# Moving the front's share, one wait and one PSUM place beside the first half of a plain MLP

## The chip, the cores and the metric

The kernel runs on one core of a Trainium2 chip, in fp32. The metric is the device time in microseconds. "Before" is the median of three runs; a profile is one further execution, whose time is given apart.

## The reference, cut to what matters

There are two stages. The first is a lightning attention with decay (4 batches, 8 heads, 768 positions, 64 wide); its output, with the heads side by side, is x (4, 768, 512). The second mixes x by a Fourier transform and applies an MLP:

```python
X = np.fft.fft(x, axis=1); X = np.fft.fft(X, axis=2)
u = x + np.real(X)
un = (u - mean(u)) / np.sqrt(var(u) + 1e-06)      # over the 512 channels
out = u + np.maximum(un @ w_ch1, 0.0) @ w_ch2     # 512 -> 2048 -> 512
```

The MLP's weights arrive as 64-bit floats.

## The kernel before

**The front.** For each batch b, `front(b)` runs `attn(b)` and then `fft_ln(b)`. The attention takes six chunks of 128 positions: k, q and v are loaded on SyncE's (SP's) DMA queue, transposed on TensorE (PE; L314, L319), scores are made (L338) and masked with the decay on VectorE (DVE; L343), the state is updated (L358, L363), and the output is made (L373, L379) and turned back (L395). `fft_ln` folds the sequence by symmetry on DVE (the sets fe and fo), transforms it on PE (L603, five groups, evicted by ScalarE (ACT) at L607), transforms the channels in three blocks `wide(1)`, `wide(2)`, `wide(0)` (L615 to L620), adds the result to x (L691 to L695), takes the statistics (L634, L635; L638 and L639 on GpSimd (POOL)) and normalizes (L655). Groups of 256 positions are named (b, g).

**The MLP.** The first four groups in `PLAIN`, (0,1), (0,2), (0,0), (1,1), are done plainly in `mlp`: their normalized rows are transposed on PE (L660), the first layer is L749 (a row is four matmuls into one PSUM place), its relu is L757 on ACT or L755 on DVE, the second layer is L763 over the pieces fc of the inner dimension. The first three groups are done in two halves of fc, 0 to 7 and then 8 to 15. After the first half the partial result is added into u (x in the code; L792, L793), at the end y is made (L796, L797) and stored (L736 on SP's queue, L738 on POOL's). Of the other eight groups (`LATE`) the normalized rows are transposed on DVE (L668) and stored to memory (L672, four DMAs for a tile, on SP), and u as well (L678). `late()` does them by a two-level Strassen form: first layer L1022, its first pair of groups being loaded into ur by `load_u` (L888, ACT's queue), with input sums sx (L923 to L929), then L1106 and L1180.

**The weights.** `load_weights` (L214 to L235) loads a raw piece of 512 columns on SP (L214) and makes fp32 of it: L226, L230, L232, L234, L235 on DVE, L225 and L228 on ACT. There are 32 pieces. The raw tiles share a ring of four ("hr") with the relu results. After the front, `combine_weights` makes the sums of weights that the Strassen form needs (L836 on DVE).

**PSUM.** While front and plain MLP run, `pa` has five places for the front, `pm` three for the MLP. In the first half of group (0,1) the two tiles of the second layer are started before the last piece fc = 7 and stay open (`split`), while the next group's first layer begins (`behind`).

**The order.** All of this is written as generators that yield an estimated cost in us after each step. `beside` and `weave` interleave two generators so that the second one advances in a set proportion to the first's costs; `chain` runs several one after the other. The program order so obtained is then adjusted by the tile scheduler, which gives instructions under `tc.high_priority` an earlier place and leaves those under `keep_in_program_order`. The stretch of interest is the end of the kernel function (L1360 to L1385): the first halves of the three groups run beside the second half of the weights' work and beside `fr`, the remaining front (the rest of attention and transform of batch 1, then batches 2 and 3). The last argument of the outer `beside` is the amount of `fr` that should pass during that first half. What remains of `fr` is then woven with `back`, the second halves and group (1,1). At `front_end.close()` the front's buffers are given up, and `load_u(0)` and the weight sums come beside the remainder of `back`. In `fft_ln(1)` (`b - 1 in LEADS` holds for b = 1 alone), a yield after the folds, 23.0, says how much other work is to pass before the transform L603 begins.

Of the kernel before, what the change touches and what calls it, by code (L numbers as in the profile page):

```python
# [17 lines left out]
ALU = mybir.AluOpType  # L18
# [59 lines left out]
def kernel(  # L78
# [12 lines left out]
    DM = H * D  # L91
# [8 lines left out]
    HM = DM // 2  # L100
# [39 lines left out]
    def new(pool, shape, tag, **kw):  # L140
        cnt[0] += 1
        return pool.tile(shape, F32, tag=tag, name=f"{tag}{cnt[0]}", **kw)

    def psum_a(shape):
        return new(pa, shape, "pa")

    def psum_m(shape):
        return new(pm, shape, "pm")
# [46 lines left out]
    NW = 2 * KO * DFF // WP  # L195
# [44 lines left out]
    def weights():  # L240

        for h in range(2):
            for f in range(h * DFF // 2, (h + 1) * DFF // 2, WP):
                for c in range(KO):
                    yield from load_weights(w1[:, c, f:f + WP], w1v[:, c, f:f + WP])
            for c in range(h * FO // 2, (h + 1) * FO // 2):
                yield from load_weights(w2[:, c, :], w2v[:, c, :])
# [47 lines left out]
    LEADS = (0,)  # L295
# [210 lines left out]
    def fold_a(b):  # L506
        for a, n in enumerate(BLK):
            yield from fold_x(b, a, n, 1, eo[b][a][1][0:n, 1, 0:DM], xn_[b, HC + a][0:n])
# [38 lines left out]
    def fold_b(b, sets):  # L547

        tt = nc.vector.tensor_tensor
        for a, n in enumerate(BLK):  # L550
            yield from fold_x(b, a, n, 0, xs[b, a][0:n], xs[b, HC + a][0:n])
            e, o = eo[b][a]
            nc.scalar.copy(e[0:n, :, HM:HM + 1], e[0:n, :, DM - 1:DM])

            am, bm = e[0:n, :, W:2 * W], o[0:n, :, W:2 * W]
            lo, hi = e[0:n, 0, 0:HM + 1], e[0:n, 1, 0:HM + 1]
            tt(am[:, 0, 0:HM + 1], lo, hi, op=ALU.add)
            tt(am[:, 1, 0:HM + 1], lo, hi, op=ALU.subtract)
            yield 0.8

            lo, hi = am[:, :, 0:QM], am[:, :, HM:QM:-1]
            tt(e[0:n, :, 0:QM], lo, hi, op=ALU.add)
            tt(e[0:n, :, QM:HM], lo, hi, op=ALU.subtract)
            yield 0.8
            lo, hi = o[0:n, 0, 1:HM], o[0:n, 1, 1:HM]
            tt(bm[:, 0, 1:HM], lo, hi, op=ALU.subtract)
            tt(bm[:, 1, 1:HM], lo, hi, op=ALU.add)
            yield 0.8
            lo, hi = bm[:, :, 1:QM + 1], bm[:, :, HM - 1:QM - 1:-1]
            tt(o[0:n, :, 0:QM], lo, hi, op=ALU.subtract)  # L570
            tt(o[0:n, :, QM:HM], lo, hi, op=ALU.add)
            yield 0.8
            sets.append((e, o))
        eo.pop(b)
# [3 lines left out]
    def fft_ln(b):  # L578
# [7 lines left out]
        if b in LEADS:  # L586
            yield from fold_a(b)
            yield from fold_b(b, sets)
            yield 2.0
        else:  # L590
            yield 1.0
            run(fold_a(b))
            yield 6.0 if b - 1 in LEADS else 3.0
            run((folds_apart if b > 1 else fold_b)(b, sets))
            yield 23.0 if b - 1 in LEADS else 9.0


        for i in (0, 1, 4, 2, 3):
            ps = psum_a([128, 2, NK])
# [133 lines left out]
    def store(b, T, y, cols=slice(0, DM)):  # L733
        if T < HC:
            row = S * b + 128 * T
            nc.sync.dma_start(out_low[row:row + 128, cols], y[:, cols])  # L736
        else:
            nc.gpsimd.indirect_dma_start(out=out_high,  # L738
                                         out_offset=row_of(2 + HC * (b + 1) + T - HC),
                                         in_=y[:, :], in_offset=None)  # L740

    def mlp(b, g, f0=0, f1=FO, behind=None):

        ut = uts[b, g]
        hr = []
        for fc in range(f0, f1):
            ps = psum_m([128, G * 128])
            for c in range(KO):
                nc.tensor.matmul(ps, lhsT=w1[:, c, 128 * fc:128 * fc + 128], rhs=ut[:, c, :],  # L749
                                 start=(c == 0), stop=(c == KO - 1))  # L750
            if fc % 4 == 0:
                hr.append(new(hp_, [128, 4, G * 128], "hr"))
            t = hr[-1][:, fc % 4, :]
            if fc % 2 and f1 == FO:
                nc.vector.tensor_scalar(t, ps, 0.0, None, op0=ALU.max)  # L755
            else:
                nc.scalar.activation(t, ps, AF.Relu)  # L757
            yield 1.7
            if f0 == 0:
                next(held.pop((b, g, fc), iter(())), 0)  # L760

        def second(ps, i, fc):
            return nc.tensor.matmul(ps, lhsT=hr[(fc - f0) // 4][:, fc % 4, 128 * i:128 * i + 128], rhs=w2[:, fc, :],  # L763
                                    start=(fc == f0), stop=(fc == f1 - 1))

        split = {}
        if behind is not None:
            for i in range(G):
                split[i] = psum_m([128, DM])
                for fc in range(f0, f1 - 1):  # L770
                    second(split[i], i, fc)
                    if fc % 4 == 3:
                        yield 3.4
                        if i == 1:
                            next(held.pop((b, g, FO), iter(())), 0)
                yield 2.6
                yield next(behind)
        for i in range(G):
            T = TT[g][i]
            if i in split:  # L780
                ps = split[i]
                tc.keep_in_program_order(second(ps, i, f1 - 1))
            else:
                ps = psum_m([128, DM])
            for fc in range(f0, f1) if i not in split else ():
                second(ps, i, fc)
                if fc % 4 == 3 and fc < f1 - 1:
                    yield 3.4
            u = xs[b, T]
            tt = nc.vector.tensor_tensor  # L790
            if f1 < FO:
                tt(u[:, 0:HM], ps[:, 0:HM], u[:, 0:HM], op=ALU.add)  # L792
                tt(u[:, HM:DM], ps[:, DM - 1:HM - 1:-1], u[:, HM:DM], op=ALU.add)  # L793
            else:
                y = new(up, [128, DM], "y", bufs=1)
                tt(y[:, 0:HM], ps[:, 0:HM], u[:, 0:HM], op=ALU.add)  # L796
                tt(y[:, HM:DM], ps[:, HM:DM], u[:, DM - 1:HM - 1:-1], op=ALU.add)  # L797
                store(b, T, y)
            yield 3.4 if i not in split else 0.8
# [517 lines left out]
    def front(b):  # L1317
        yield from attn(b)
        yield from fft_ln(b)

    def weave(lead, other, ratio):

        t_lead = t_other = 0.0
        for d in lead:
            t_lead += d
            while t_other < t_lead * ratio:
                d = next(other, None)
                if d is None:
                    return t_lead + sum(lead)
                t_other += d  # L1330
                yield d
            yield d
        return t_lead

    def run(gen):
        return sum(gen)

    def part(gen, n):
        for d in gen:
            yield d  # L1340
            n -= d
            if n <= 0:
                return

    def chain(gens):
        for g in gens:
            yield from g

    w = weights()
# [4 lines left out]
    def beside(lead, t, other, t_other):  # L1354
        return weave(lead, part(other, t_other), t_other / t)

    att1, mix = attn(1), fft_ln(0)
    att0 = attn(0)
    run(part(att0, 2.7))
# [3 lines left out]
    run(beside(mix, 24.0, beside(att1, 2.75 * t_chunk, w, 0.16 * NW), 0.16 * NW + 1.75 * t_chunk))  # L1363

    half = [[mlp(b, g, h * FO // 2, (h + 1) * FO // 2) for b, g in PLAIN[:3]] for h in range(2)]
    half[0][0] = mlp(*PLAIN[0], 0, FO // 2, half[0][1])
    fr = chain([att1, fft_ln(1)] + [front(b) for b in range(2, B)])
    t_rest, t_back = 3 * t_front - 5 * t_chunk, len(PLAIN) * t_mlp - 50.0
    t_half = 1.5 * t_mlp
    run(beside(beside(chain(half[0]), t_half, w, 0.5 * NW), t_half + 0.5 * NW, fr, t_rest * t_half / t_back))  # L1370
    run(w)
    back = chain(half[1] + [mlp(*PLAIN[3])])
    run(weave(fr, back, (t_back - t_half) / (t_rest - t_rest * t_half / t_back)))
    front_end.close()
# [44 lines left out]
```

## Time and profile before

| | |
|---|---|
| median of three runs | 789.23 us (788.49 to 789.73) |
| profiled execution, its own time | 789.55 us |
| its span in the profile | 787.6 us |
| mean granted TensorE clock | 0.992 |
| TensorE busy | 755.3 us, 96% |
| VectorE busy | 602.9 us, 77% |
| ScalarE busy | 230.7 us, 29% |
| GpSimd busy | 177.2 us, 22% |
| chain that ended last | PE 79%, DVE 9%, DMA 6% |

Columns of a group or a step in the trace: where it starts, how long it takes, the engine, the line, the operation, the tile written, the tiles read, shapes, and in brackets the engine's idle time ahead of it and what ended that. "x3" after a step stands for three instructions that follow one another and are shown as one. In the rows of tenths each of the 40 digits stands for 19.7 us of the span. The costliest single groups are L749 (119.6 us of PE) and L763 (115.4 us).

### The profile page before, as it was taken

The numbers are of one execution on the slowest core, as the hardware profiler recorded it, in microseconds if no ns is written. First come the engines' busy times: TensorE is split into PE (matmuls) and PEld (weight loads), VectorE is DVE, ScalarE is ACT, GpSimd is POOL, SyncE is SP. The second block draws the span as 40 slices with busy tenths as digits, with TensorE's granted clock in tenths as the row PEclk, the third lists the DMA queues.
The fourth block names the chain that finished last, engine by engine and source line by source line (L and its number), as shares of the span: only waits on it lengthen the run. The fifth ranks groups of instructions, "written<-read, shape, count | busy, mean of one in ns | idle before, by whom it ended". The sixth has DMA issues, their size and how long they took to land.

```text
span 787.6 us, 15005 instructions
## 1 busy us (share of the span) xinstructions
PE 755.3 (96%) x5784; PEld 648.0 (82%) x5784; DVE 602.9 (77%) x1167; ACT 230.7 (29%) x532; POOL 177.2 (22%) x202
## 2 busy tenths in 40 slices
PE   6888999999999999999995999999999999999997
PEld 5777876777685858678744889999999999999997
DVE  6999999767824686236597999878987699758984
ACT  3755444415531212231100221023411342024310
POOL 3223330001112014120003960350014100230013
PEclk9999999999999999999997999999999999999999
DMA  9979633246734037931243363776455455455442
GB/s 232 261 168 252 192 113 113 76 133 151 211 83 140 29 72 211 237 97 46 72 100 96 136 235 125 249 246 214 150 162 157 147 186 182 121 187 175 133 140 78
DMA packets 152957, 120.23 MB, mean 153 GB/s; under 512 B 114238, under 2 KB 114622, under 8 KB 152886
## 3 DMA queue, kind: packets, MB, share of 16 engines
q1 hardware_dynamic: 145824, 100.51, 45.9%
q0 software_dynamic: 4032, 12.99, 4.7%
q10 hardware_dynamic: 3030, 5.78, 2.1%
q8 instruction: 46, 0.75, 0.4%
q14 instruction: 25, 0.20, 0.1%
HBM read 88.04 MB, written 31.20 MB: 151 GB/s over the span
## 4 chain that ended last, share of the span: by engine, by line
PE 79%; DVE 9%; DMA 6%; issue 2%; ACT 1%; POOL 1%; SPq 1%; ACTq 0%; DVEq 0%; POOLq 0%
PE p L1180 21%; PE p L1106 17%; PE pm L749 11%; PE pm L763 9%; PE p L1022 6%; PE pa L338 3%; PE pa L379 3%; PE pa L603 3%; DMA raw<-in_moe_w_ch_dram 2%; PE pa L373 2%; DMA ur<-utd 1%; PE pa L358 1%; PE pa L314 1%; PE pa L319 1%; PE pa L395 1%
## 5 line engine op out<-in xcount | busy, mean ns | idle before, releaser
L749 PE MATMUL pm<-ut,w 128*128 128x256 f32 x512 | 119.6, 382 | 2.5 <-DVE x L793 1.4
L763 PE MATMUL pm<-w,hr 128*128 128x512 f32 x256 | 115.4, 595 | 0.0
L749 PEld LDWEIGHTS pm<-ut,w 128*128 128x128 f32 x512 | 94.3, 190 | 18.2 <-issue 3.7
L763 PEld LDWEIGHTS pm<-w,hr 128*128 128x128 f32 x256 | 46.7, 190 | 48.7 <-issue 48.0
L1201 POOL TENSOR_TENSOR y<-y,u 128x512 f32<-128x512 f32 x12 | 19.9, 1661 | 186.8 <-DVE y L1210 155.5
L1180 PE MATMUL p<-tx,sx 128*128 128x128 f32 x400 | 52.7, 275 | 0.0
L1180 PEld LDWEIGHTS p<-tx,sx 128*128 128x128 f32 x400 | 48.6, 192 | 0.0
L1115 DVE TENSOR_TENSOR ha<-p,ha 128x512 f32<-128x512 f32 x60 | 40.0, 683 | 8.3 <-PE p L1106 8.1
L310 POOL TENSOR_TENSOR kd<-k,decay 128x512 f32<-128x512 f32 x20 | 21.7, 1083 | 107.7 <-PE pa L358 71.7
L1186 ACT COPY y<-p 128x128 f32<-128x128 f32 x48 | 12.8, 266 | 103.6 <-PE p L1180 103.1
L343 DVE TENSOR_TENSOR sc<-pa,decay 128x512 f32<-128x512 f32 x48 | 31.0, 683 | 15.0 <-PE pa L338 14.6
L1188 DVE TENSOR_TENSOR y<-p,y 128x128 f32<-128x128 f32 x92 | 25.4, 283 | 16.1 <-PE p L1180 9.4
L1180 PE MATMUL p<-w,ha 128*128 128x128 f32 x288 | 37.4, 275 | 0.0
L638 POOL TENSOR_SCALAR ve<-mv 128x2 f32<-128x2 f32 x12 | 5.9, 491 | 133.5 <-DVE mv L635 133.2
L1115 DVE TENSOR_TENSOR hs<-p,hs 128x512 f32<-128x512 f32 x39 | 26.1, 683 | 12.0 <-PE p L1106 12.0
L1180 PEld LDWEIGHTS p<-w,ha 128*128 128x128 f32 x288 | 34.9, 192 | 0.1
L338 PEld LDWEIGHTS pa<-qT,kT 64*128 64x128 f32 x384 | 25.1, 193 | 12.0 <-ACT qT L321 6.7
L757 ACT ACTIVATE hr<-pm 128x256 f32<-128x256 f32 x44 | 16.7, 382 | 58.9 <-PE pm L749 54.8
L1106 PE MATMUL p<-sx,tx 128*128 128x128 f32 x264 | 33.9, 275 | 0.0
L338 PE MATMUL pa<-qT,kT 64*128 64x128 f32 x384 | 30.1, 292 | 2.9 <-ACT qT L321 2.9
L1106 PEld LDWEIGHTS p<-sx,tx 128*128 128x128 f32 x264 | 31.7, 192 | 0.0
L379 PE MATMUL pa<-sc,v 128*64 128x128 f32 x384 | 28.6, 282 | 1.1 <-DVE sc L343 1.1
(270 smaller groups left out, 1740.3 us busy)
## 6 DMA issues: line engine op xcount, KB each, us to landing
tx<-td SPq DMA_DIRECT2D x84, 256.0 KB
raw<-in_moe_w_ch_dram SPq DMA_DIRECT2D x32, 512.0 KB
tx<-sd SPq DMA_DIRECT2D x63, 256.0 KB
k<-in_k_dram SPq DMA_DIRECT2D x24, 256.0 KB
q<-in_q_dram SPq DMA_DIRECT2D x24, 256.0 KB
v<-in_v_dram SPq DMA_DIRECT2D x24, 256.0 KB
td<-tx SPq DMA_DIRECT2D x21, 256.0 KB
ud<-x SPq DMA_DIRECT2D x16, 256.0 KB
```

The lines of the kernel that those rows point to most:

```text
L310: nc.gpsimd.tensor_tensor(kd, kt, kpow, op=ALU.mult)
L338: mm(pss[hi][:, hp, :], lhsT=kT[HD[hi], hp, :], rhs=qT[HD[hi], hp, :], start=True, stop=True)
L343: nc.vector.tensor_tensor(t, pss[hi], decay[:, hi::2, :], op=ALU.mult)
L379: mm(po[HD[hi], hp, :], lhsT=vt[:, 2 * hp + hi, :], rhs=sc[hi][:, hp, :], start=(c == 0 and hp == 0), stop=(hp == HP - 1), skip_group_chec ...
L603: mm = nc.tensor.matmul(ps[:, n, :], lhsT=piece(a, i, n), rhs=cs[0:rows, a, i in (2, 3), n, :], start=(a == 0), stop=(a == 1))
L749: nc.tensor.matmul(ps, lhsT=w1[:, c, 128 * fc:128 * fc + 128], rhs=ut[:, c, :], start=(c == 0), stop=(c == KO - 1))
L763: return nc.tensor.matmul(ps, lhsT=hr[(fc - f0) // 4][:, fc % 4, 128 * i:128 * i + 128], rhs=w2[:, fc, :], start=(fc == f0), stop=(fc == f ...
L1022: nc.tensor.matmul(ps, lhsT=s2.A[a][:, kt, 128 * i:128 * i + 128], rhs=U[b][:, kt, :], start=(first and kt == 0), stop=(kt == 1), skip_gro ...
L1106: nc.tensor.matmul(ps[:, 128 * i:128 * i + 128], lhsT=ab[m][0][:, 128 * i:128 * i + 128], rhs=ab[m][1], start=(start and i == 0), stop=Tru ...
L1115: V.tensor_tensor(o, p, o, op=ADD)
L1180: nc.tensor.matmul(ps[:, 0:HM // 2], lhsT=ab[m][0][i], rhs=ab[m][1][:, i, :], start=(start and i == 0), stop=(i == HF // 2 - 1), skip_grou ...
L1188: V.tensor_tensor(o, ps[:, 0:HM // 2], o, op=ADD)
```

## The change

Four edits. The share of `fr` beside the first half of the MLP is raised by 15.0, the unit being the estimated us of the yields. The yield ahead of the transform of batch 1 goes from 23.0 to 27.0. The second of the two open tiles of group (0,1) gets a place in the front's PSUM pool `pa` in place of one in `pm`. And the partial sums of these two tiles (L792, L793) are given a higher priority in the scheduler.

```diff
@@ fft_ln, ahead of the transform
-            yield 23.0 if b - 1 in LEADS else 9.0
+            yield 27.0 if b - 1 in LEADS else 9.0
@@ mlp, the open tiles
-                split[i] = psum_m([128, DM])
+                split[i] = (psum_m, psum_a)[i]([128, DM])
@@ mlp, the partial sums
             if f1 < FO:
-                tt(u[:, 0:HM], ps[:, 0:HM], u[:, 0:HM], op=ALU.add)
-                tt(u[:, HM:DM], ps[:, DM - 1:HM - 1:-1], u[:, HM:DM], op=ALU.add)
+                with tc.high_priority(200) if i in split else ExitStack():
+                    tt(u[:, 0:HM], ps[:, 0:HM], u[:, 0:HM], op=ALU.add)
+                    tt(u[:, HM:DM], ps[:, DM - 1:HM - 1:-1], u[:, HM:DM], op=ALU.add)
@@ the share
-    run(beside(beside(chain(half[0]), t_half, w, 0.5 * NW), t_half + 0.5 * NW, fr, t_rest * t_half / t_back))
+    run(beside(beside(chain(half[0]), t_half, w, 0.5 * NW), t_half + 0.5 * NW, fr, t_rest * t_half / t_back + 15.0))
```

Lines after the edit in `mlp` stand one lower in the changed kernel (L793 for L792, L1023 for L1022).

## The prediction

> **What bounds the kernel now.** I read the page first, then TensorE's waits, then windows of 20 us, then the sequence of instructions at the two largest waits.
>
> ```profile
> span 787.6 us, 15005 instructions
> ...
> PE 755.3 (96%) x5784; PEld 648.0 (82%) x5784; DVE 602.9 (77%) x1167; ACT 230.7 (29%) x532; POOL 177.2 (22%) x202
> ...
> PE   6888999999999999999995999999999999999997
> ...
> PEclk9999999999999999999997999999999999999999
> ```
>
> TensorE (PE) is busy 96% of the span, so only its idle time, 32 us, and time at a lower clock can be won. One slice stands out, the twenty-second (about 413 to 433 us): half idle, and at 0.7 of the clock. TensorE's waits say which idle time is whose:
>
> ```profile
> PE p L1022 <- DVE sx L925: 8.3, 1, 8.3
> ...
> PE pm L749 <- DVE x L793: 1.4, 1, 1.4
> ...
> PE p L1180 <- DVE y L1188: 1.3, 1, 1.3
> ...
> PE pm L749 <- ACT hr L757: 1.1, 1, 1.1
> ...
> PE pa L660 <- DVE un L655: 0.7, 1, 0.7
> ```
>
> (Columns: total us, times, longest us.) Up to 110 us the change moves nothing. From there on the trace has 13.34 us of PE gaps over 0.3 us: 1.43 at 132.34, 0.65 at 153.56, 1.11 at 255.87, 0.49 at 364.97, 8.33 at 417.27, 1.33 at 514.06. The largest is the seam between the front with the plain MLP and the Strassen part:
>
> ```profile
> 400.00:420.00 20.00, 17.27 (x45) 8.11 (x43) 20.00 (x24) 0.37 (x1) 0.00 (x0) 1.00 0.32 66
> 420.00:440.00 20.00, 14.40 (x56) 12.35 (x57) 13.90 (x23) 3.00 (x8) 13.50 (x12) 0.75 0.38 136
> ```
>
> (Columns: window, length, busy of PE, PEld, DVE, ACT, POOL, clock, DMA.) Before 420 us VectorE (DVE) has not an idle moment while PE runs dry; after it the clock drops. The sequence:
>
> ```profile
> 391.35 24.20 PE L763 MATMUL pm<-w,hr 128*128 128x512 f32 x56
> 399.49 2.36 DVE L836 TENSOR_TENSOR w1s<-w 128x1024 f32<-128x1024 f32 x2 [1.13 <-POOL rs L639]
> 420.75 0.45 SPq L736 DMA_DIRECT2D out_dram<-y  x1
> 423.38 0.42 DVE L796 TENSOR_TENSOR y<-pm,x 128x256 f32<-128x256 f32 x1 [1.90 <-DMA out_dram<-y]
> 425.60 2.04 PE L1022 MATMUL p<-sx,w1s 128*128 128x256 f32 x4 [8.33 <-DVE sx L925]
> ```
>
> The front's last PE instruction ends at 391.35. Its tail on DVE, the weight sums L836, the last y and the input sums L923/L925 then take until 425.46. PE has only the plain MLP's remainder (28 blocks of four L763 left, 24.1 us) and 1.7 us of L1022 on stored inputs to lay beside 34.1 us of DVE work: 34.1 - 25.9 = 8.2, the gap seen. The cure would be more MLP work left when the front ends, which is the front's share.
>
> **What the change moves, part by part.** The instruction order of the changed kernel, compared engine by engine, has the same 5784 matmuls; nothing is added or removed.
>
> *The share (+15.0) and the wait 27.0.* The front runs ahead of the plain MLP sooner. After the front's last PE instruction there now come three L749 rows and 32 L763 blocks instead of 28 L763 blocks. A row is four matmuls of 0.43 us, 1.73; a block of four L763 is 3.44, or 0.86 each, so 5.2 + 27.5 = 32.7 us against 24.1. Measured from a point that both orders share, the last L620 of the second wide block (ends 384.57), PE had 32.7 us of work and now has 39.7; DVE needs 40.9 us to sx, now up to 41.6, since two L755 relus (0.41 each) move behind that point. Gap: 40.9 to 41.6 less 39.7, so 1.2 to 1.9. I take 1.5. It cannot reach zero: the last y adds follow the last L763 and sx follows them, 0.7 + 1.4 + 0.3 of latency against 1.7 of cover, 0.6. The cover for everything DVE does there is these 35 rows and blocks; without it the 8.33 come back. What is late next is the store of y: it is issued on SP behind the last four transposed stores (L672, 0.63 each) and two of L678 as before (420.75, landed 2.5 us later, L796 waited 1.90). It sits inside the DVE figure. Behind the seam GpSimd's sums (5.64 us a round) stay under PE's round (6.03), so the gain is carried to the end.
>
> *The clock.* The granted clock was 0.5 from 419.90 to 430.14; 4.54 us of matmuls fell into it after 425.60, at twice their time: 2.27 us lost. Gaps of 1.43, 1.39 and 1.11 left the clock at 1.00. The Trainium skill ("TensorE: Matmul & The Clock Gate", Part 1, "The HAM clock gate") has about 3.4 us of busy time at half clock before full speed returns: an estimate of 1.7 lost. The row decides, 2.27. With a gap of 1.5 it is all won; with one over some 3 us it stays (here the drop came 2.6 us after PE went idle).
>
> A rule on the same page speaks against the change: "A second HAM failure mode: psum-queue depth-cycling" has PE's frequent micro-idles while it cycles through PSUM banks make the clock fall and rise again. The change trades one long gap for several short ones. By the rule each burst could cost what the seam's did, 2 us, twice or three times; by the rows (full clock through every gap of 0.4 to 1.43 from 13.7 to 419.9) nothing. I take nothing.
>
> *The PSUM place and the priority.* With two open second-layer tiles in pm's three places, L749 of the next group waits for the adds, and DVE has these among weight steps that wait for their data (1.30 idle for raw at 130.65, first add at 131.93, second at 133.20). The tile now lies in pa, the adds come ahead of those steps: 1.43 to 0. The front has four places of five meanwhile. Each L603 group is 1.31 us on PE and its eviction 0.52 on ACT, so four are enough: 0, at most one eviction (0.5). The adds themselves (four of 0.42) delay weight steps by at most 1.7 us.
>
> *The weight steps.* DVE does its L226 to L235 in order, and behind a raw load that hasn't landed stands all else. Six steps now lie between the halves of un in the norm of batch 1 where one lay: 6 x 0.42 to 0.69, some 2.5, plus 0.4 for un against 1.3 us of PE cover: 1.5 for a gap that was 0.65. The first half of un: 0.2.
>
> *Queues.* The first raw loads of the second half of w2, issued on SP at 168.68 and 170.29 between the front's stores, now come behind 16 stores of L672 (0.63 to 0.67 each, some 10.5 us). On SP the k, q, v loads of batch 2 stand behind raw, and raw waits for a ring place which PE frees. From both sides: none of it late (their slack is some 0.7 to 1.4 us where nearest), or each of four pairs of raw late by 2.5 us, 10 in all. I take the near end, as the trace's raw waits at DVE in this region are of the size 1.3: score waits of 0.6 and 0.2 in chunks 0 and 3, k of the fourth chunk 0.7, raw at qs and sc 0.5; sum 2.0, range 0 to 10.
>
> *Elsewhere.* The wait of 1.11 at 255.87 (L749 for a relu on ACT) goes: 15.5 us of PE work now covers 13.6. The 0.49 at 364.97 becomes 0.2. The 1.33 at 514.06 is untouched.
>
> **The sum.** Profiled execution 789.55, span 787.6. Won: 1.43 + 1.11 + (8.33 - 1.5 = 6.83) + 2.27 + 0.29 = 11.93. Lost: 0.85 + 0.2 + 2.0 = 3.05. Net 8.9, so 780.65 in such an execution; the median of the runs was 0.32 below the profiled one: **780.3**.
>
> **Rivals.**
>
> *The seam moves only half.* DVE does its tail later than I count, since steps which lay in the earlier MLP stretch now fall behind the last L620, or the y store comes later on SP. For it: that chain runs through DVE, a DMA of 2.5 us and SP. Against: the order of SP's tail is the same, and only two L755 are added. Then a gap of 4 to 5 remains and with it the slow clock: 789.2 - 3.8 - 2.8 (the two small gaps and the 0.29) + 3.05 = 785.6.
>
> *All small gaps vanish.* The raw loads and k are in time: 780.3 - 3.05, and the seam at its floor of 0.6, another 0.9: 776.4. For it: slacks counted from one execution are of the size of the waits.
>
> *Slower: the late raw loads.* One mechanism, at 160 to 300 us: raw behind 16 stores on SP, DVE in order at L226, and k, q, v of batch 2 behind raw, so PE stands before L338 and L603. Price: four pairs of raw, 2.5 us each make 10, and with one long enough to halve the clock 2.3 more. It decides once these waits exceed 2.0 + 8.9 = 10.9, near 2.7 a pair: 791 to 793 at 3 to 3.5. Against it: the late pieces are of w2's second half, which PE needs only in the second half of the MLP, and PE has MLP rows in between.
>
> *It doesn't do what it says.* The front ends no earlier because it waits for DVE, not for its share: 1.43 alone goes and the waits are paid: within 0.2% of 789.
>
> **How the numbers follow.** 0.2% (1.6 us) is about what a measurement of this kernel can tell from no change. Likeliest, 777.5 to 783.5: 0.55. Seam half, 783.5 to 787.5: 0.19. Below 777.5: 0.08. Within 0.2%: 0.06. Slower: 0.12. Faster is the sum of the first three, 0.82. The range takes the likeliest, most of the seam case and half of the best one: 776.4 to 787.0.
>
> **What would show it.** The L1022 wait for sx at 1 to 2 us, and PEclk at 9 throughout slices 20 to 23: seam and clock right; a wait of 4 or more: the first rival. No L749 wait for L793: the PSUM place. Waits of L660, L338, L314 or L363's readers between 150 and 300 us summing to some 3: the weight steps and queues; over 10: the slower case. A second stretch of half clock anywhere proves the rule on micro-idles against my reading of the rows.

## The result, and the profile after

| | before | changed |
|---|---|---|
| median of five runs | 788.78 us (788.40 to 789.73) | 775.63 us (774.72 to 776.28) |
| profiled execution | 789.55 us | 774.72 us |
| its span | 787.6 us | 772.9 us |
| mean granted TensorE clock | 0.992 | 0.999 |

The ratio is 0.9831, with a 95% interval of 0.9817 to 0.9845: 13.15 us faster by the medians. The forecast was 780.3, a gain of 8.9, with a range down to 776.4; the measured time lies 0.8 us below that range. The two profiled executions differ by 14.83, more than the medians. The parts below are read from these two, so their sum carries 1.7 us that belong to the two executions.

The page after, the same lines as before the change (span, busy times, PE and its clock in tenths of forty slices):

```profile
span 772.9 us, 14999 instructions
...
PE 752.0 (97%) x5784; PEld 646.6 (84%) x5784; DVE 602.9 (78%) x1167; ACT 230.5 (30%) x532; POOL 177.6 (23%) x202
...
PE   6889999999999999999999999999999999999997
...
PEclk9999999999999999999999999999999999999999
```

The hole in the twenty-second slice is filled and the clock has no dent. VectorE is busy for 602.9 us as before: nothing was made cheaper, it was laid elsewhere. TensorE's waits of the changed kernel, from 110 to 520 us (total, times, longest):

```profile
PE p L1023 <- DVE sx L926: 1.3, 1, 1.3
PE pa L660 <- DVE un L655: 1.0, 1, 1.0
PE p L1181 <- DVE y L1189: 0.6, 1, 0.6
```

Those are all. The waits of L749 are gone, the seam is at 1.3, L660 went from 0.7 to 1.0. No wait for a k load or a score is there. The windows around the seam, and its sequence:

```profile
400.00:420.00 20.00, 18.66 (x62) 11.45 (x61) 16.41 (x25) 1.87 (x5) 5.36 (x6) 1.00 0.34 91
420.00:440.00 20.00, 20.00 (x95) 17.50 (x94) 19.69 (x27) 4.87 (x13) 19.45 (x15) 1.00 0.39 146
```

```profile
383.16 27.73 PE L763 MATMUL pm<-w,hr 128*128 128x512 f32 x64
...
409.12 0.45 SPq L736 DMA_DIRECT2D out_dram<-y  x1
...
411.73 0.42 DVE L797 TENSOR_TENSOR y<-pm,x 128x256 f32<-128x256 f32 x1 [1.90 <-DMA out_dram<-y]
...
413.96 1.10 PE L1023 MATMUL p<-sx,w1s 128*128 128x256 f32 x4 [1.34 <-DVE sx L926]
```

The chain on VectorE and SP is the old one, down to the wait of 1.90 for y's store. It runs 11.6 us earlier (411.73 for 423.38), since the front ends earlier. TensorE's L763 give way to the first L1022 only 4.7 us earlier (410.7 for 415.4), since more MLP work is left. The difference, 7.0, is what the gap has lost.

Where the 14.64 us between the ends of TensorE's work in the two executions come from, cut at instructions that both have (the fourth stretch ends at the first L1180 that reads tx):

| stretch | before | changed | difference | of it in gaps |
|---|---|---|---|---|
| up to the first L749 | 96.23 | 95.18 | -1.05 | -1.0 |
| front beside the MLP, to the first L1022 | 319.16 | 315.55 | -3.61 | -2.55 |
| seam, to the first L1022 that reads sx | 10.21 | 3.23 | -6.98 | -6.99 |
| first layer behind it (the clock) | 50.78 | 48.55 | -2.23 | 0 |
| rest | 306.39 | 305.62 | -0.77 | -0.77 |

The first row is spread between executions: the stretch, which the change does not reorder, took 94.4 to 98.7 us in the profiles below. The same holds for the last row: its wait at L1181 ends with work on VectorE that a load had held up, and was between 0.5 and 1.2 in them. Those two rows make 1.8 us.

### The profile page after: what moved, and what is told of

The parts are those of the page before. It is cut to its first block, busy times and chain, and to the rows that moved or that the text cites. A ratio compares the mean times of both kernels' runs of the same rounds, so it can differ in the third digit from the quotient of the medians.

```text
span 772.9 us, 14999 instructions
## 1 busy us (share of the span) xinstructions
PE 752.0 (97%) x5784; PEld 646.6 (84%) x5784; DVE 602.9 (78%) x1167; ACT 230.5 (30%) x532; POOL 177.6 (23%) x202
## 4 chain that ended last, share of the span: by engine, by line
PE 82%; DVE 10%; DMA 3%; issue 1%; ACT 1%; SPq 1%; POOL 1%; DVEq 0%; ACTq 0%; POOLq 0%
PE p L1181 21%; PE p L1107 17%; PE pm L749 13%; PE pm L763 9%; PE p L1023 6%; PE pa L603 3%; PE pa L338 3%; PE pa L379 2%; PE pa L373 2%; PE pa L314 1%; PE pa L358 1%; PE pa L395 1%; PE pa L763 1%; DMA raw<-in_moe_w_ch_dram 1%; PE pa L319 1%
## 5 line engine op out<-in xcount | busy, mean ns | idle before, releaser
L749 PE MATMUL pm<-ut,w 128*128 128x256 f32 x512 | 118.3, 381 | 0.0
L763 PE MATMUL pm<-w,hr 128*128 128x512 f32 x240 | 109.0, 596 | 0.1
L749 PEld LDWEIGHTS pm<-ut,w 128*128 128x128 f32 x512 | 94.7, 190 | 14.4 <-issue 2.7
L763 PEld LDWEIGHTS pm<-w,hr 128*128 128x128 f32 x240 | 43.6, 190 | 44.5 <-issue 42.8
L1181 PE MATMUL p<-tx,sx 128*128 128x128 f32 x400 | 52.7, 275 | 0.0
L1181 PEld LDWEIGHTS p<-tx,sx 128*128 128x128 f32 x400 | 48.6, 192 | 0.0
L1181 PE MATMUL p<-w,ha 128*128 128x128 f32 x288 | 37.4, 275 | 0.0
L1116 DVE TENSOR_TENSOR hs<-p,hs 128x512 f32<-128x512 f32 x39 | 26.1, 683 | 12.4 <-PE p L1107 12.4
L338 PEld LDWEIGHTS pa<-qT,kT 64*128 64x128 f32 x384 | 25.1, 193 | 12.2 <-ACT qT L321 6.4
L1181 PEld LDWEIGHTS p<-w,ha 128*128 128x128 f32 x288 | 34.9, 192 | 0.1
L338 PE MATMUL pa<-qT,kT 64*128 64x128 f32 x384 | 30.1, 292 | 2.9 <-ACT qT L321 2.9
```

The source lines that it names most:

```text
L338: mm(pss[hi][:, hp, :], lhsT=kT[HD[hi], hp, :], rhs=qT[HD[hi], hp, :], start=True, stop=True)
L1116: V.tensor_tensor(o, p, o, op=ADD)
L1181: nc.tensor.matmul(ps[:, 0:HM // 2], lhsT=ab[m][0][i], rhs=ab[m][1][:, i, :], start=(start and i == 0), stop=(i == HF // 2 - 1), skip_grou ...
```

## The experiments

Twelve runs of eleven kernels, each timed in five rounds against the kernel before. Times are medians; the interval of a ratio in what follows is the 95% one. The stated work after the last L620 is the sum of the L749 and L763 matmuls left at 0.43 and 0.86 us each. (In the traces each of these matmuls has two records, so x64 stands for 32.)

**The share alone.**

```diff
-    ... fr, t_rest * t_half / t_back))
+    ... fr, t_rest * t_half / t_back + 15.0))
```

> The kernel before with the share raised by 15.0 and nothing else. Its order leaves 24 L749 matmuls and 32 L763 on TensorE after the last L620, 37.9 us, against 27.5 before and 34.4 in the changed kernel. Theory A (the time is the sum of TensorE's gaps, and the seam's gap is about 35.8 us less that work, not below 0.6): seam 0.6 to 0.8, full clock there, so 789 - 7.6 - 2.3 = 779 or a little less, with the wait of L749 for the partial sums (1.4) still there. Theory B (the gain came mostly from the PSUM place and the priority, or from work that overlaps better along the whole front): 784 or more.

Measured: 776.69, ratio 0.9853 (0.9830 to 0.9876). The seam's gap is 1.28 and the clock is full throughout. The share alone brings 12.1 of the 13.15 us. Theory B falls. The wait for the partial sums, expected to stay, is absent, though neither PSUM place nor priority is there. One L749 waits 0.72 for a relu instead, at 349.97. The seam, with more TensorE work than the changed kernel has, isn't at 0.6: the sums of a first tile (L1046) had come in between the two input sums on VectorE.

**The share and the yield, without place and priority.**

> Share +15.0 and the yield 27.0, without the PSUM place and without the priority. Work after the last L620 as in the changed kernel (34.4). Theory A: seam 1.3, full clock, and the 1.4 wait for the partial sums is back: 775.6 + 1.4 = 777.0. Theory B: 781 or more.

Measured: 778.04, ratio 0.9867 (0.9842 to 0.9892). The time is 1.0 above theory A's figure, and the 1.4 which that figure was made of isn't there. The sequence around the partial sums in this kernel:

```profile
130.05 1.99 PE L749 MATMUL pm<-ut,w 128*128 128x256 f32 x8
...
131.88 2.79 PE L603 MATMUL pa<-cs,fe 128*128 128x193 f32 x16
132.97 0.42 DVE L792 TENSOR_TENSOR x<-pm,x 128x256 f32<-128x256 f32 x1
134.24 0.42 DVE L793 TENSOR_TENSOR x<-pm,x 128x256 f32<-128x256 f32 x1
134.81 1.97 PE L749 MATMUL pm<-ut,w 128*128 128x256 f32 x8
```

VectorE's adds are as late as before, 1.3 us apart among the weight steps. But between the two L749 rows there are now 16 instructions of L603 (2.8 us) where there were 8 (1.5 us), and the view shows no idle time ahead of the row. Share and yield together took this wait away by putting one more group of L603 in front of the row. With the share alone one more such group also lies between the last L763 of the open tiles and the row, and there the adds follow one another (134.10 and 134.43), so which of the two ended the wait in that kernel isn't shown.

**Place and priority alone.**

```diff
-                split[i] = psum_m([128, DM])
+                split[i] = (psum_m, psum_a)[i]([128, DM])
...
-                tt(u[:, 0:HM], ps[:, 0:HM], u[:, 0:HM], op=ALU.add)
+                with tc.high_priority(200) if i in split else ExitStack():
+                    tt(u[:, 0:HM], ps[:, 0:HM], u[:, 0:HM], op=ALU.add)
```

> The kernel before with only the PSUM place and the priority; share and yield as before, so the seam has 27.5 us of TensorE work after the last L620 and keeps its gap of 8.3 and the half clock. Theory A (these two edits are worth the 1.43 wait of L749 for the partial sums and no more): 787.4, the wait gone, the seam at 8.3. Theory C (the wait is covered by whatever order the share gives, and the edits only move it): 788.5 to 789.2. Theory B (they carry a good part of the gain): under 785.

Measured: 788.18, ratio 0.9993 (0.9973 to 1.0013), no difference that can be told. The waits:

```profile
PE p L1023 <- DVE sx L926: 8.3, 1, 8.3
PE pm L749 <- ACT hr L757: 1.6, 1, 1.6
...
PE pa L660 <- DVE un L655: 0.7, 1, 0.7
...
```

The 1.4 of L749 for L793 is gone, and the next wait, L749 for a relu, has grown from 1.1 to 1.6. So these edits do what was said of them, some 0.9 us net by this profile, and the seam doesn't move.

**The changed kernel without the place.**

> The changed kernel with the second open tile back in pm. The adds come early by their priority. Theory A: L749 waits at most some tenths for the adds: 775.6 to 776.3. If the place is what ends the wait: 777.0, with a wait of L749 for L794 of about 1.4.

Measured: 776.69, ratio 0.9848 (0.9822 to 0.9873).

**The changed kernel without the priority.**

> The changed kernel without the priority: the adds lie among the weight steps again, but the second tile doesn't hold a place of pm. Theory A: no wait at L749 or one under 0.5: 775.6 to 776.3. If the order of the adds is what ends the wait: 777.0. Against share_wait (778.04), which lacks both, this and the run without the place tell which of the two is worth anything.

Measured: 777.12, ratio 0.9855 (0.9827 to 0.9883). Neither profile has a wait at L749. TensorE's stretch from the first L749 to the first L1022 takes 315.67 and 315.54 us, as in the changed kernel (315.55); with both left out it is 316.58. One of the two seems to be enough for about 1 us, but the intervals overlap and the times can't settle it.

**The yield left at 23.0.**

> The changed kernel with the yield left at 23.0: 37.9 us of TensorE work after the last L620 in place of 34.4, so the seam is bound by the last L763, then y and sx (1.28 in the run with the share alone). Theory A: seam 1.3 as in the changed kernel, time 775.2 to 776.5; the yield of 27.0 by itself takes work away from the seam and is worth nothing there. If the yield pays in the transform of batch 1: 777.5 or more, with new waits between 120 and 160 us.

Measured: 775.85, ratio 0.9835 (0.9809 to 0.9860), the same as the changed kernel. The seam is 1.28, and one L749 waits 0.62 for a relu. The yield of 27.0 isn't needed beside this share.

**The yield without the share.**

> The changed kernel without the +15.0: the yield 27.0 then leaves 24.1 us of TensorE work after the last L620, 3.4 less than before. Theory A: a gap of about 11.7 at the seam, half clock, and the place and the priority give about 1: 791. If the yield helps in front of the transform by more than it costs at the seam: 788 or less.

Measured: 790.90, ratio 1.0029 (1.0012 to 1.0045), slower than before. TensorE's waits from 110 to 520 us:

```profile
PE p L1023 <- DVE sx L926: 12.1, 1, 12.1
...
PE pa L603 <- DVE fe L526: 0.7, 1, 0.7
```

Almost every other wait of the front is gone here, L660's too, and still the kernel is slower: the yield lets MLP work pass ahead of the transform, which is then missing at the seam. 3.4 us less work there made 3.8 more gap.

**A share of 12.**

```diff
-    ... fr, t_rest * t_half / t_back + 15.0))
+    ... fr, t_rest * t_half / t_back + 12.0))
```

> The changed kernel with +12.0 in place of +15.0: 31.0 us of TensorE work after the last L620, 3.4 less. Theory A: the seam's gap grows from 1.3 to 4.8; at that length the clock falls as it did before, some 2 us more: 781. If the clock does not fall at 4.8 us: 779. Theory B (the seam's length is not what sets the time): within 1 us of 775.6.

Measured: 781.56, ratio 0.9912 (0.9896 to 0.9929). The time was right for a wrong reason: the gap is 3.09, not 4.8, and in the profiled execution the clock stayed full. The gap fell short of 4.8 because only TensorE's side had been counted: VectorE needed 36.4 us from the last L620 to sx here, and 38.5 in the changed kernel, where two more halves of un, a relu and an addition lay behind that L620. Less these 2.1 us, 4.8 would have been 2.7. The other runs of it were 2.8 to 4.9 us longer. A fallen clock doesn't explain all of that: three of them have the profiled one's mean granted clock of 0.999. Nor is the seam all that a share of 12 costs: it makes 1.75 of the 5.9 us, and the front's stretch was 1.2 to 2.7 us longer in the two profiles of this kernel.

**The same kernel again.**

> The kernel of share_12 once more. Its profile had a gap of 3.1 at the seam at full clock and 778.56, its other runs lay at 781.3 to 783.5. If a gap of this length loses the clock in some executions and not in others[...]: again two groups of times some 2 to 3 us apart, and a profile that shows either 3.1 at full clock or half clock with L1023 matmuls under it. If that was only the spread of the early loads: times spread evenly, and the profile again at full clock.

Measured: 781.56, ratio 0.9905 (0.9884 to 0.9927). The gap is 3.09 again, and now the clock fell. The same window in both profiles, the earlier first (length, busy times, then the clock, DMA share and GB/s):

```profile
412.00:426.00 14.00, 10.91 (x49) 8.92 (x49) 10.41 (x16) 2.25 (x6) 7.68 (x7) 1.00 0.37 128
```

```profile
412.00:426.00 14.00, 10.91 (x39) 8.26 (x38) 8.41 (x15) 1.64 (x5) 6.62 (x7) 0.88 0.38 123
```

Equal busy time, ten matmuls fewer in it. The granted clock was 0.5 for 3.41 us, from 419.46, and the first layer's stretch behind the seam took 50.22 in place of 48.55: 1.67 us. The same gap thus costs 3.1 or 4.8. The Trainium skill ("TensorE: Matmul & The Clock Gate", Part 1, "The HAM clock gate") calls the activity window free-running and the number of slow matmuls at a start run-variable, with about 3.4 us before the full clock; that agrees with the 3.41 here, and half of it is the 1.7 measured. That the place in the window also decides whether a gap of 3.09 loses the clock isn't shown. The times did not fall into two groups, so how often it happens stays open.

**A share of 20.**

```diff
-    ... fr, t_rest * t_half / t_back + 15.0))
+    ... fr, t_rest * t_half / t_back + 20.0))
```

> The changed kernel with +20.0: 36.2 us of TensorE work after the last L620 in place of 34.4. Theory A: the seam is then bound by the last L763, y and sx, 1.28, so nothing is left to win by the share: 775.2 to 776.2. If the share still pays: 774.5 or less, with the seam under 1.

Measured: 778.59, ratio 0.9866 (0.9846 to 0.9887). Here both views fail. The seam shrinks to 0.54, the floor that the prediction worked out, and the kernel is slower than with 15.0:

```profile
PE pa L603 <- DVE fe L526: 1.2, 2, 0.7
...
PE pm L763 <- DVE hr L755: 0.7, 1, 0.7
PE p L1023 <- DVE sx L926: 0.5, 1, 0.5
```

The stretch of the front is 318.65, 3.1 more than with 15.0. Two waits of L603 for the folds and one of L763 for a relu make 1.9 of it; the rest is busy time and gaps under 0.5. In this order TensorE comes to the transform of the last batch before VectorE has the folds.

**Every front store of batch 1 issued twice.**

```diff
                         nc.sync.dma_start(dst, src)
+                        if b == 1:
+                            copy = dram.tile([128, KO, G * 128], F32, name=f"cp{g}{i}{r}")
+                            dst = copy[:, :, 0:32].rearrange("(a d) c n -> d c a n", d=32)
+                            nc.sync.dma_start(dst, src)
```

> The changed kernel with every L672 store of batch 1 issued a second time, to a scratch place in memory: 16 more issues of 0.65 us on SP, some 10 us, ahead of the raw loads of w2's second half and of the k, q, v loads of batch 2, which is twice the suspected cost. If the queue has only the 1 us of slack that the prediction took (so that late raw and k loads were to cost 2.0 us, and more when later): TensorE waits before L314, L338 or L363's readers of 5 to 9 us, 781 to 785. If the slack is large, the reason why these 2.0 us didn't come: 775.6 to 776.6, and SP's queue simply later.

Measured: 784.97, ratio 0.9955 (0.9936 to 0.9974), 9.3 us over the changed kernel. SP's queue and the next instruction of TensorE:

```profile
187.56 1.04 SPq L214 DMA_DIRECT2D raw<-in_moe_w_ch_dram  x2
188.71 0.38 SPq L303 DMA_DIRECT2D k<-in_k_dram  x1
...
191.88 0.43 DVE L226 TENSOR_SCALAR e<-raw 128x512 uint16<-128x512 uint16 x1 [10.40 <-DMA raw<-in_moe_w_ch_dram]
...
194.78 1.09 PE L314 MATMUL pa<-ident,k 128*128 128x128 f32 x4 [6.55 <-DMA k<-in_k_dram]
```

TensorE waits 6.55 for the first k of batch 2, behind raw, and the clock is then halved from 191.85 to 198.68; 3.9 us of that lie under work, some 2 us lost. This is the stretch of the prediction's slower rival (at L314, not L338 and L603), and near its price of 10 us and 2.3 for the clock. VectorE waits 10.4 us at L226 for raw, and no wait of TensorE for VectorE is added: of the two mechanisms that the prediction gave that rival, only the loads behind raw are real here.

**Half of these stores twice** (condition `b == 1 and i == 0`).

> The changed kernel with half of the L672 stores of batch 1 issued twice: 8 more issues on SP ahead of raw, k, q and v, some 5.2 us in place of the 9.7 us of the run with all of them. There the first k of batch 2 made TensorE wait 6.55, so its slack should be 3.2; in the changed kernel's trace k was in use by GpSimd 3.4 us ahead of L314. If slack is what hid the cost: a wait of 1.6 to 2.0 at L314, full clock, 777.2 to 777.8. If the stores cost by their traffic and not by their place in the queue: half of the whole run's loss, 4.5, so 780.

Measured: 782.16, ratio 0.9899 (0.9871 to 0.9926), with its runs between 778.97 and 784.06. The wait is 3.13, more than expected:

```profile
188.29 0.38 SPq L303 DMA_DIRECT2D k<-in_k_dram  x1
...
194.39 0.63 PE L314 MATMUL pa<-ident,k 128*128 128x128 f32 x4 [3.13 <-DMA k<-in_k_dram]
```

In the changed kernel k was issued at 179.00 and GpSimd used it at 184.98:

```profile
179.00 0.38 SPq L303 DMA_DIRECT2D k<-in_k_dram  x1
...
184.98 1.06 POOL L310 TENSOR_TENSOR kd<-k,decay 128x512 f32<-128x512 f32 x1 [1.86 <-DMA k<-in_k_dram]
...
188.41 0.60 PE L314 MATMUL pa<-ident,k 128*128 128x128 f32 x4
```

Taken from the first L749 of each execution (95.18, 94.85, 97.87), k was issued 10.0 us later in the full run and 6.6 in the half one. Less the waits of 6.55 and 3.13, both leave 3.5 us of slack, and the trace of the changed kernel shows 3.4 (188.41 - 184.98). The load itself took as long in all three (5.98, 6.07 and 6.10 us from its issue to the first use that waited for it), so it is the place in the queue that cost, not the added traffic. The miss of this expectation lay in the delay (6.6 for the 5.2 taken). The half run's median loses 6.5 us, but its runs differ by their clock. The two with a mean granted clock of 1.0 took 778.97 and 779.32, 3.3 and 3.7 us over the changed kernel, which the 3.1 at k and the 0.4 at the seam (1.74), as profiled, account for. The other four, at 0.992 to 0.998, took 781.2 to 784.1. The profiled execution is one of these, and its clock was halved for 3.41 us from 195.77, behind the wait for k, and before that here:

```profile
33.86 0.66 PE L395 MATMUL pa<-ident,ds 128*128 128x128 f32 x4 [1.55 <-ACT ds L388]
```

```profile
36.00:40.00 4.00, 4.00 (x42) 3.60 (x40) 3.04 (x8) 2.08 (x5) 0.00 (x0) 0.50 0.94 236
```

The half clock lasted 6.83 us, from 35.34, and no gap near it was longer than these 1.55. The same wait was 1.58 in two other kernels, and in the kernel without the priority a gap of 2.69 ended at 54.47, all at full clock.

## Why the prediction was wrong, point by point

**Right: the seam and the clock.** The seam's gap was put at 1.5 with 1.2 to 1.9 around it, and is 1.34; the gain of 6.83 is 6.99. The clock was to give 2.27 by the row and 1.7 by the Trainium skill ("TensorE: Matmul & The Clock Gate", Part 1, "The HAM clock gate"); it gave 2.23, so the row was the better guide. Those two are 9.2 of the 13.15 us. The chain into the seam passes through the store of y on SP, as said: VectorE waits 1.90 us for it before and after. The "blocks of four" that the prediction counts there are single matmuls of 0.86 us; its sums are right. The dose was tried from both sides:

| TensorE work after the last L620, us | kernel | seam's gap, us |
|---|---|---|
| 24.1 | yield without share | 12.12 |
| 27.5 | before | 8.33 |
| 31.0 | share 12 | 3.09 |
| 34.4 | changed | 1.34 |
| 36.2 | share 20 | 0.54 |
| 37.9 | share alone | 1.28 |

The last row isn't lower than the one above it because L1046 came in between on VectorE.

**Right, with another cause: the wait of 1.43.** It is gone, but the share alone takes it away as well. The PSUM place and the priority were credited with 1.43; alone they end that wait and give 0.6 (not told from nothing). Beside the share they give 0.8 (yield at 23.0) to 2.4 us (yield at 27.0) by medians whose intervals overlap, of which the front's stretch shows 0.4 and 1.0. That this term came out was luck in part. The place cost the front nothing that a trace shows.

**Right: the waits at 255.87 and 364.97** went (1.11 and 0.49, against 1.11 and 0.29).

**Wrong: the steps "weight steps" and "queues", 3.05 us lost.** The changed trace has 0.35 of it, at L660 (0.65 to 1.00). The norm's gap was put at 1.5 and 0.2 more for its first half: VectorE had 3.2 us from the first to the second half of un (149.33 to 152.53), near the count, but TensorE had L660 and L763 to do in it and stood for 1.00. The queue term, 2.0, was nothing at all. It took slacks of 0.7 to 1.4 and let late raw and k loads spend them. The raw loads did come later, as told (177.84 for 168.68), but VectorE's waits for raw between 110 and 300 us grew only from 2.2 to 3.4, and no wait of TensorE shows them. The k loads were misread. In the kernel before, the first k of batch 2 stood behind the same 16 stores (eight from 163.19, eight here):

```profile
179.51 6.01 SPq L672 DMA_DIRECT2D utd<-e  x8
...
187.42 0.38 SPq L303 DMA_DIRECT2D k<-in_k_dram  x1
...
192.74 1.07 POOL L310 TENSOR_TENSOR kd<-k,decay 128x512 f32<-128x512 f32 x1 [1.78 <-DMA k<-in_k_dram]
...
197.91 0.60 PE L314 MATMUL pa<-ident,k 128*128 128x128 f32 x4
```

It was there 5.2 us ahead of L314, not 0.7 to 1.4. In the changed kernel it is issued 8.4 us earlier (179.00) and used 9.5 us earlier, so 3.4 us were left, by the trace and by both doubled runs. The next chunk's k had 1.8 (GpSimd uses it at 195.21, L314 at 197.05). The rival built on the same queue was thus about rightly priced, and too near: for the first k it starts only when SP is a further 3.5 us late. Where it starts for the next chunk wasn't tried.

**Not foreseen.** The prediction held that only idle time and a lower clock could be won. But TensorE's busy time from the first L749 to the seam fell by 1.06 us (315.47 to 314.41), most of it in L749 (113.5 to 112.4) and in L603 on fe (12.4 to 11.8), with L763 0.6 longer. The number of instructions is the same, so this is how they follow one another; it wasn't taken apart, and in the other kernels with the full clock in this stretch its busy time lies between 314.4 and 316.3 us. L1181's wait fell by 0.77 and the first 95 us by 1.05, both within what executions of other kernels show in the same place.

**The sum.** From the forecast 8.9: 2.70 for waits that were not there, 0.16 at the seam, -0.04 for the clock, 0.20 at the wait of 364.97, 1.06 of busy time, and 1.82 for the first and last rows of the table make 14.8, the 14.83 of the two profiled executions. By the medians 13.15 is left, so most of the 1.82 is not the change's. The step that failed is the loss of 3.05; with 0.35 in its place the forecast would have been 777.6, inside the range and 2 us from the truth.

**The range** ended at 776.4 with the case that every small wait vanishes. That was very nearly the case that came, and it had a chance of 0.08. Its weight was too small: each of the four terms of the queue's 2.0 was an estimate of slack from a neighbouring wait, and none had a wait of its own in the trace.

**Rule and rows on the clock.** In the changed kernel gaps up to 1.34 left the clock at 1.00, as the rows of before said. The fall that the Trainium skill ("TensorE: Matmul & The Clock Gate", "A second HAM failure mode: psum-queue depth-cycling") ties to frequent short idle times did not come there. But the sign that the prediction named against its own reading, a second stretch of half clock, did come in one profile, that of the half-doubled stores: 6.83 us after a gap of no more than 1.55, while 2.69 went by at full clock in another kernel. So at these lengths a single gap's length doesn't decide, and whether the rule on short idle times does stays open. At 3.09 the kernel with a share of 12 showed both.

No kernel tried was faster than the changed one. The share with place and priority but the yield at 23.0 equals it.

## What to carry to other kernels

At a seam between two stages, count the work left on each engine behind the last instruction that both stages share. With both engines counted anew the stall came within 0.2 us (1.5 for 1.34); with one engine's side taken over from another order it was missed by 1.7 (4.8 for 3.09). The balance also tells how far a share can be moved before the stall only changes its place. A wait that you can't find in a trace should be costed by the time between the landing of its data and their use, read from that trace, and not by a wait nearby. And an edit that removes a short wait may find it gone already, when another edit of the same change puts work in front of it.

## What the runs showed of the hardware

The stretches of half clock that lay wholly within a trace were 3.41, 6.83 and 10.24 us long, one, two and three times 3.41. An idle time of 3.09 led to one of them in one execution and to none in another of the same kernel; the fall came after work had resumed, at 419.46 for a gap that ended at 418.71. One stretch followed a gap of 1.55, while a gap of 2.69 in another kernel was followed by none. An L672 store held SP's queue for 0.57 to 0.94 us, mostly 0.63, and a load behind 16 more of them was issued 10.0 us later.
